# Tile 0's norm on all partitions by halves in a three-stage kernel: float32 products with ones, and reordered start steps

## The chip, the cores and the metric

The kernel runs on one core of a Trainium2 chip. The metric is the time of one execution on the device in microseconds. Engines are named as the profile names them: PE is TensorE (PEld its weight loads), DVE is VectorE, ACT is ScalarE, POOL is GpSimd, SP is SyncE, whose queue issues most DMAs.

## What is computed

Three stages follow each other: a chunked scan over four sequences with eight heads (768 tokens, 32 values a head, a state of 16), a gated feed-forward network with an RMS norm ahead of it (256 to 1536 and back), and a second network with mixed neighbours, squared ReLU and a sigmoid gate. Cut to what matters here:

```python
def _attn_ref(x, a, B, C):
    ...
        cum = np.cumsum(la, axis=-1)
        L = np.exp(cum[:, :, :, None] - cum[:, :, None, :])
        M = np.einsum('bhin,bhjn->bhij', Cc, Bc) * (L * causal)
        y_intra = np.einsum('bhij,bhjd->bhid', M, xc)
    ...

def _moe_ref(x, w_gate, w_val, w_out, rms_g):
    rms = np.sqrt(np.mean(x * x, axis=-1, keepdims=True) + 1e-06)
    xn = x / rms * rms_g
    g = xn @ w_gate
    silu = g * (1.0 / (1.0 + np.exp(-g)))
    val = xn @ w_val
    return (silu * val @ w_out).astype(np.float32)
```

All inputs and outputs are float32.

## The kernel before

The 3072 tokens go through in six tiles of 512, a tile being 128 positions of all four batches. The kernel keeps activations transposed: 128 features on partitions, 512 tokens along the row. A matrix product is made of three float32r products (`mm3`, L746): high weights by high activations, low by high, high by low; so each weight is converted, cast to a high part and differenced to a low one (`convert`, L253: `move` on DVE, two ACT steps in `magnitude`, `merge` on DVE, casts on ACT and differences on DVE in `parts`). Weights come in pairs of jobs, each pair a DMA into a `wst` tile; the casts' outputs are `wgh`, `wgl`, `wvh`, `wvl`, `woh`, `wol`.

Before the first feed-forward product of tile 0 there is a start of some 25 us. For tile 0 and tile 1 the decay matrices `E` are made on the chip: a product with an identity (`spread_eye`, L376) and a spread product with `wvvh` and `wkh` (`spread_e`, L385, the tiles are borrowed from later weights) fill a bank `Eb`, and ACT takes its exponential (`exp_e`, L399). Score products `sc` (`scores`, L468) times `E` give the mask products `M` on DVE (`mask`, L509); `M` times `x` gives `y` for one batch (`y_mm`, L536). Then comes tile 0's norm, and with it the normalised activations `xn`.

The norm of tile 0 before the change (L641 to L737): after each batch ACT squares `y` (`sq`), and two float32 products of `sq`'s columns as weights with one column of ones put the sums of 128 tokens into one column of a bank `ss`: the tokens are then on partitions. For two batches together (a half, `cols[h]`), ACT takes Ln, Exp and Square of two columns (`rms_a`, L688), DVE refines the inverse root in a Newton step (`rms_rest`, `rms_b`), and TensorE spreads each column over all partitions by a float32 product with an identity (L720). Behind the spreads of a half stands one filling product (`fill`, L635) whose result is not used. `xn_f` (L725) multiplies by the weights `g_v` and the spread factor out of the bank, `xn_split` makes the high and low parts.

`ffn1` (L752) takes tile 0's first two units (`HALVED`) in halves of 256 tokens: 48 half-width products, then units of 12 full products each, `g` and `v`, into the four banks of the pool `pmm`; ACT takes the Silu of `g` (`sl`), DVE multiplies by `v` (`hf`), and the contraction products `x` run two units behind. The attention of tile 1 runs between: `y_two` (L563) multiplies the state by `Ch`, which DVE has scaled in `ch_mul` (L495).

The order is made in two steps. `START` (L40) names the start's steps in the order in which their instructions are recorded: `e0` and `e2` exponentials of two batches, `s0` and `s1` scores, `m` masks, `y` product and square of a batch, `n` norm of a half, `c` and `P` steps of the first weight pair, `z` the next pair, `x0`, `x2` tile 1's exponentials, `S0` and `M` its scores and masks, `q0`, `q1` the identity products ahead of the first spread. A planner (`Order`, L1140) then runs all instructions through a model of engines, queues and buffers, by rank, with those of some steps marked urgent, and `arrange` (L1364) fixes each engine's order by what it found. A step that moves in `START` so moves instructions on all engines, far behind it too.

Of the kernel before, what the change touches and what calls it, by code (L numbers as in the profile page):

```python
# [9 lines left out]
F32 = mybir.dt.float32  # L10
# [3 lines left out]
AF = mybir.ActivationFunctionType  # L14
ALU = mybir.AluOpType

P = 128
NB, NH, S, D, N = 4, 8, 768, 32, 16
# [3 lines left out]
T = NB * P  # L22
# [14 lines left out]
        (99, 99, 99, 99, 99, 99, 99, 99, 99, 99, 99, 99, 99))  # L37

HIGH_ACT = ((0, 1, 2, 3, 4, 5, 6, 7, 10, 11), (2, 7))
START = 's0 k0 q0 q1 l0 p0 e0 l1 p1 m0 m1 e2 s1 m2 m3 y0 y1 y2 n0 c0 c1 P0 y3 x0 x2 d0 L0 u0 L1 n1 P1 z0 t0 S0 M1 k1 M0'  # L40
SPARE, LATE_E, BEHIND = ((0, 0), (0, 1), (1, 0)), (), (('n0', 'n1'),)
LOW_POOL, ON_POOL = (), ()

SUB_DVE, MIX_UNIT = tuple(range(27)), 9
MEANS, SPREAD, LOAD_E = (6, 10), 11, (3, 6)
WARM, COLD, HALVED, FILL = (9,), 11, 2, {('n', 0): 1, ('n', 2): 1}

TABLES = {AF.Ln: "natural_log_exp_and_others", AF.Exp: "natural_log_exp_and_others",
          AF.Silu: "silu_and_others", AF.Sigmoid: "sigmoid_and_others"}
# [28 lines left out]
def tile_kernel(ctx: ExitStack, tc, a_c, x_t, B_t, B_s, C_s, B_p, C_p, C_h, kc,  # L78
                w_gate, w_val, w_out, w_k, w_v, w_r, out):
    nc = tc.nc  # L80
    slots, chains, groups, gates, urgent, ranks, costs = {}, [], [], [], [], {}, {}
# [13 lines left out]
    rp = Pool("rp", 1)  # L95
    dp = ctx.enter_context(tc.tile_pool(name="dp", bufs=1, space=bass.MemoryType.DRAM))
    pacc = Pool("pacc", 2, bass.MemoryType.PSUM)
    pmm = Pool("pmm", 4, bass.MemoryType.PSUM)
    patt = Pool("patt", 2, bass.MemoryType.PSUM)
    vec_e, act_e, pool_e = nc.vector, nc.scalar, nc.gpsimd  # L100

    def t2(name, dt=F32, tag="t2"):
        return rp.tile([P, T], dt, tag=tag, bufs=5, name=name)
# [12 lines left out]
    def f32(ap):  # L116
        return ap.bitcast(F32)
# [27 lines left out]
    last = [None, None]  # L145
# [11 lines left out]
    def kcol(j):  # L157
        return k_sb[:, j:j + 1]
# [3 lines left out]
    ones = wp.tile([P, P], F32R, name="ones")  # L162
# [59 lines left out]
    for q in range(NU // 2):  # L222
        s = slice(2 * P * q, 2 * P * (q + 1))
# [81 lines left out]
    A = {c: {} for c in range(NC + 2)}  # L305
# [70 lines left out]
    def spread_eye(c, b):  # L376
        for half in range(2):
            pool, tag = (pacc, "acc") if c and b in LATE_E else (pmm, "mm")
            ps = A[c]["Eb", b, half] = pool.tile([P, T], F32, tag=tag, name="Eb")
            mm = nc.tensor.matmul(ps, eye, before.unsqueeze(1).broadcast_to([P, 4, P]), start=True, stop=False)  # L380
            if len(costs) < COLD:
                costs[mm.ins.name] = 427.0
            A[c]["eye", b, half] = mm.ins.name
# [171 lines left out]
    def columns_of(c, s):  # L555
        t = A[c]["yT"]
        if c:
            return t[:, :, s]
        return t.rearrange("p s (a i) -> p s a i", a=2)[:, s.start // (2 * P)]
# [67 lines left out]
    tiny = rp.tile([P, 4, P], F32, tag="Bs", bufs=1, name="tiny")  # L627
# [4 lines left out]
        nc.gpsimd.affine_select(out=eye_f, in_=eye_f, pattern=[[1, P]], base=0, channel_multiplier=-1,  # L632
                                compare_op=ALU.not_equal, fill=1.0)

    def fill(ps, n, behind):  # L635
        for k in range(n):
            mm = nc.tensor.matmul(ps, f32(ones), f32(ones).unsqueeze(1).broadcast_to([P, 2, P]), start=True, stop=True, skip_group_check=True)
            costs[mm.ins.name] = 430.0
            chains.extend((one, mm.ins.name) for one in behind)

    def square0(b):  # L641
        d = A[0]
        if b % 2 == 0:
            q = rp.tile([P, T], F32, tag="Ch", bufs=1, name="sq") if b else t2("sq")
            d["q", b // 2] = q.rearrange("p (a i) -> p a i", a=2)
            pool, tag = (patt, "at") if b else (pmm, "mm")
            d["ss", cols[b // 2].start] = pool.tile([P, T], F32, tag=tag, name="ss")
        fill(d["ss", cols[b // 2].start][:, :2 * P], FILL.get(("y", b), 0), d["last", b])
        i = slice(b % 2 * P, b % 2 * P + P)
        q, ss = d["q", b // 2][:, :, i], d["ss", cols[b // 2].start]  # L650
        nc.scalar.activation(out=q, in_=d["y", b][:, :2 * P].rearrange("p (a i) -> p a i", a=2), func=AF.Square)
        for j in range(2):
            nc.tensor.matmul(ss[:, T - NB + b:T - NB + b + 1], q[:, j], f32(ones)[:, 0:1], start=j == 0, stop=j == 1)

    def rms_sq(c, s, he, le):
        d = A[c]
# [31 lines left out]
    def rms_a(c, s):  # L688
        d = A[c]
        if c > 1:  # L690
            ss, r = d["ss", 0 if c else s.start][:, s], d["rs", 0 if c else s.start][:, s]
            ms, w = (t2(n)[:, s] for n in ("ms", "nw"))
        else:
            b = slice(s.start // P, s.stop // P)
            ss = d["ss", 0 if c else s.start][:, T - NB:][:, b]
            r, ms, w = (tiny[:, 1, 16 * c + 4 * k:16 * c + 4 * k + 4][:, b] for k in range(3))
        d["nw", s.start] = ss, r, ms, w
        tabled(out=r, in_=ss, func=AF.Ln, scale=1.0 / DM, bias=kcol(EPS))
        if c:
            rms_rest(c, s)  # L700
        tabled(out=r, in_=r, func=AF.Exp, scale=-0.5)
        tabled(out=w, in_=r, func=AF.Square)

    def rms_rest(c, s):
        ss, _, ms, _ = A[c]["nw", s.start]
        nc.vector.tensor_scalar(out=ms, in0=ss, scalar1=1.0 / DM, scalar2=1e-6, op0=ALU.mult, op1=ALU.add)

    def rms_b(c, s):
        d = A[c]
        _, r, ms, w = d.pop(("nw", s.start))  # L710
        nc.vector.scalar_tensor_tensor(out=w, in0=w, scalar=-0.5, in1=ms, op0=ALU.mult, op1=ALU.mult)
        nc.vector.scalar_tensor_tensor(out=r, in0=w, scalar=1.5, in1=r, op0=ALU.add, op1=ALU.mult)
        if c <= 1:
            if c:
                d["rs", 0 if c else s.start] = pmm.tile([P, T], F32, tag="mm", name="rb")
            else:
                d["rs", 0 if c else s.start] = d["ss", 0 if c else s.start]
            for k in range(s.stop // P - s.start // P):
                b = s.start // P + k if c else k
                mm = nc.tensor.matmul(d["rs", 0 if c else s.start][:, b * P:b * P + P], r[:, k:k + 1].broadcast_to([P, P]), eye_f,  # L720
                                 start=True, stop=True)
            if c == 0:
                fill(d["rs", s.start][:, 2 * P:], FILL.get(("n", s.start // P), 0), [mm.ins.name])

    def xn_f(c, half, s):  # L725
        d = A[c]
        if ("xnf", half) not in d:
            d["xnf", half] = t2("xnf")
        f = d["xnf", half, s.start] = d["xnf", half][:, s]
        nc.vector.scalar_tensor_tensor(out=f, in0=columns_of(c, s)[:, half], scalar=g_v[:, half:half + 1],  # L730
                                       in1=d["rs", 0 if c else s.start][:, s] if c else d["rs", 0 if c else s.start][:, :s.stop - s.start], op0=ALU.mult, op1=ALU.mult)

    def xn_split(c, half, s, he, le):
        d = A[c]
        if ("xn", half) not in d:
            d["xn", half] = pair("xn", "xn")
        split(d["xn", half][:, :, s], d.pop(("xnf", half, s.start)), he, le)  # L737

    def xn_out(c, halves, s, he, le):
        for half in halves:  # L740
            xn_f(c, half, s)
        for half in halves:
            xn_split(c, half, s, he, le)
# [146 lines left out]
    full, cols = slice(0, T), (slice(0, T // 2), slice(T // 2, T))  # L890
    nc.vector.memset(f32(ones), 1.0)

    def warm_up(n, pool, tag):
        w = pool.tile([P, T], F32, tag=tag, name="warm")
        for k in range(n):
            mm = nc.tensor.matmul(w, ones, ones.unsqueeze(1).broadcast_to([P, 4, P]), start=True, stop=True)
            if len(costs) < COLD:
                costs[mm.ins.name] = 427.0 if costs else 900.0
# [36 lines left out]
    def squares(b):  # L935
        y_mm(0, b)
        square0(b)
        y_out(0, b)

    def norms(h):  # L940
        norm0(cols[h])
# [17 lines left out]
    def late_decayed(_):  # L959
        for b in range(NB):  # L960
# [34 lines left out]
    for t in range(NC):  # L995
        c, e = t + 1, t + 2
# [105 lines left out]
        x2, tail = ffn1(t, hook)  # L1102
        if t == 0:
# [9 lines left out]
            x2 = [x2s[:, m] for m in range(2)]  # L1113
# [298 lines left out]
```

## Time and profile before

| | us |
|---|---|
| median of 3 runs | 508.67 (508.61 to 508.83) |
| profiled execution: its own time | 508.6 |
| profiled execution: span | 506.6 |
| PE busy | 500.2 (99%) |
| DVE busy | 375.7 (74%) |
| ACT busy | 307.9 (61%) |
| POOL busy | 10.4 (2%) |

The span is the time from the first instruction to the last one's end; the execution's own time has 2.0 us more around it. Busy shares are averages: in the first 30 us the engines work in a different balance from the rest, so the start is read from timelines. A matmul's end is modelled, and matmuls overlap, so the step from one's start to the next one's start tells more than its length. A float32 product stands as two records in the trace.

### The profile page before, as it was taken

What the parts mean: (1) busy time and instruction counts of PE and PEld (TensorE: products, weight loads), DVE (VectorE), ACT (ScalarE), POOL (GpSimd) and SP (SyncE); (2) the same over time, 40 slices, a digit from 0 to 9 for tenths busy, and PEclk for the clock granted to TensorE, in tenths of its full rate; (3) what the DMA queues carried; (4) which work ended last, traced back from release to release, by engine and by line L of the source; (5) the groups of instructions that cost most, each with busy time, mean ns of one, the idle gap of its engine ahead of it and who ended that gap; (6) DMA issues with size and microseconds to landing.
All of it is one profiled execution on the core that took longest, in us unless ns stands there. A gap on an engine that the chain in (4) does not pass through costs nothing.

```text
span 506.6 us, 7497 instructions
## 1 busy us (share of the span) xinstructions
PE 500.2 (99%) x2869; PEld 406.8 (80%) x2869; DVE 375.7 (74%) x610; ACT 307.9 (61%) x509; POOL 10.4 (2%) x26
## 2 busy tenths in 40 slices
PE   8999999999999999999999999999999999999997
PEld 4687887788888888888888888888888888888885
DVE  6899998988698965479995659996628763335672
ACT  5999798566589744457763456764358643345552
POOL 1100000000010000010000010000000000000000
PEclk9999999999999999999999999999999999999999
DMA  8868755342321220152111141110000000000101
GB/s 257 230 204 276 261 175 193 105 137 93 123 85 43 78 82 13 57 174 77 42 58 68 46 162 44 65 48 36 0 1 1 18 25 1 1 1 0 42 0 42
DMA packets 23283, 42.60 MB, mean 84 GB/s; under 512 B 3136, under 2 KB 6720, under 8 KB 23248
## 3 DMA queue, kind: packets, MB, share of 16 engines
q1 hardware_dynamic: 20496, 33.41, 20.0%
q10 hardware_dynamic: 2752, 8.72, 5.1%
q8 instruction: 22, 0.36, 0.3%
q14 instruction: 13, 0.11, 0.1%
HBM read 38.52 MB, written 3.34 MB: 83 GB/s over the span
## 4 chain that ended last, share of the span: by engine, by line
PE 91%; DVE 5%; ACT 2%; issue 1%; DMA 1%; DVEq 0%; ACTq 0%
PE v L748 10%; PE v L750 10%; PE v L749 10%; PE g L748 6%; PE x L748 6%; PE x L749 6%; PE x L750 6%; PE g L749 6%; PE g L750 6%; PE kp L748 4%; PE kp L750 4%; PE kp L749 4%; PE y L527 2%; PE sc L442 1%; PE rps L750 1%; PE rps L749 1%
## 5 line engine op out<-in xcount | busy, mean ns | idle before, releaser
L792 DVE TENSOR_TENSOR hf<-sl,v 128x512 f32<-128x512 f32 x72 | 49.0, 683 | 50.0 <-PE v L750 49.5
L140 ACT CAST h<-hf 128x512 fp32r<-128x512 f32 x72 | 44.4, 617 | 60.8 <-DVE hf L792 60.7
L133 ACT ACTIVATE sl<-g 128x512 f32<-128x512 f32 x72 | 42.8, 595 | 44.9 <-PE g L750 44.6
L143 DVE TENSOR_TENSOR h<-hf,h 128x512 fp32r<-128x512 f32 x72 | 50.5, 701 | 24.1 <-ACT h L140 24.1
L748 PE MATMUL g<-xn,wgh 128*128 128x512 f32 (+1 forms) x148 | 58.0, 392 | 0.4 <-DVE E L514 0.4
L749 PE MATMUL g<-xn,wgl 128*128 128x512 f32 (+1 forms) x148 | 57.0, 385 | 0.4 <-DVE wgl L289 0.4
L748 PE MATMUL v<-xn,wvh 128*128 128x512 f32 (+1 forms) x148 | 57.0, 385 | 0.0
L750 PE MATMUL g<-xn,wgh 128*128 128x512 f32 (+1 forms) x148 | 56.8, 384 | 0.0
L749 PE MATMUL v<-xn,wvl 128*128 128x512 f32 (+1 forms) x148 | 56.8, 384 | 0.0
L750 PE MATMUL v<-xn,wvh 128*128 128x512 f32 (+1 forms) x148 | 56.8, 383 | 0.0
L749 PE MATMUL x<-h,wol 128*128 128x512 f32 x144 | 56.3, 391 | 0.0
L748 PE MATMUL x<-h,woh 128*128 128x512 f32 x144 | 55.8, 391 | 0.1
L750 PE MATMUL x<-h,woh 128*128 128x512 f32 x144 | 55.2, 389 | 0.0
L867 DVE TENSOR_TENSOR k<-rl 128x512 f32<-128x512 f32 x40 | 30.0, 749 | 15.0 <-ACT rl L863 15.0
L143 DVE TENSOR_TENSOR h<-k,h 128x512 fp32r<-128x512 f32 x48 | 32.8, 686 | 10.3 <-ACT h L140 9.9
L140 ACT CAST h<-k 128x512 fp32r<-128x512 f32 x48 | 29.7, 619 | 16.5 <-DVE k L867 16.3
L748 PE MATMUL kp<-xm,wkh 128*128 128x512 f32 x96 | 37.7, 393 | 0.0
L750 PE MATMUL kp<-xm,wkh 128*128 128x512 f32 x96 | 37.4, 390 | 0.0
L749 PE MATMUL kp<-xm,wkl 128*128 128x512 f32 x96 | 37.4, 389 | 0.0
L748 PE MATMUL v<-h,wvvh 128*128 128x512 f32 x96 | 37.3, 389 | 0.0
L749 PE MATMUL v<-h,wvvl 128*128 128x512 f32 x96 | 37.3, 389 | 0.0
L863 ACT ACTIVATE rl<-kp 128x512 f32<-128x512 f32 x48 | 28.5, 594 | 14.1 <-PE kp L750 13.4
(157 smaller groups left out, 983.0 us busy)
## 6 DMA issues: line engine op xcount, KB each, us to landing
E<-la_r ACTq DMA_DIRECT2D x16, 512.0 KB
x<-in_x_t SPq DMA_DIRECT2D x6, 512.0 KB
wst<-in_w_gate SPq DMA_DIRECT2D x6, 512.0 KB
wst<-in_w_val SPq DMA_DIRECT2D x6, 512.0 KB
wst<-in_w_out SPq DMA_DIRECT2D x6, 512.0 KB
Br<-in_B_s SPq DMA_DIRECT2D x12, 256.0 KB
Cr<-in_C_s SPq DMA_DIRECT2D x12, 256.0 KB
out<-r SPq DMA_DIRECT2D x11, 256.0 KB
```

What stands on the lines that cost most here:

```text
L133: one = nc.scalar.activation(out=out, in_=in_, func=func, **kw).ins.name
L140: last[1] = nc.scalar.copy(x[:, 0, :], src).ins
L143: last[0] = le.tensor_tensor(out=x[:, 1, :], in0=src, in1=f32(x[:, 0, :]), op=ALU.subtract).ins
L442: nc.tensor.matmul(bank[:, q * 256:(q + 1) * 256], bs[:, p, :], cs[:, p, :, :].rearrange("p a i -> p (a i)"), start=True, stop=True)
L527: nc.tensor.matmul(y[half][32 * j:32 * j + 32, at[half]:at[half] + P], x[:, b, h * D:(h + 1) * D], m[:, h, :], start=start and at[half] == ...
L748: nc.tensor.matmul(ps[:, s], w[0][:, k, ws], x[:, 0, s], start=first, stop=False, skip_group_check=s.stop - s.start < T)
L749: nc.tensor.matmul(ps[:, s], w[1][:, k, ws], x[:, 0, s], start=False, stop=False, skip_group_check=s.stop - s.start < T)
L750: nc.tensor.matmul(ps[:, s], w[0][:, k, ws], x[:, 1, s], start=False, stop=last, skip_group_check=s.stop - s.start < T)
L792: nc.vector.tensor_mul(hf, sl, v)
L863: marks.append(nc.scalar.activation(out=rl, in_=kp, func=AF.Relu).ins.name)
L867: nc.vector.tensor_mul(k2, rl, rl)
```

## The change

The norm of tile 0 is made on all partitions. For each half, two float32 products of a 128 by 128 block of ones with 256 columns of squares put the sum of each token on every partition of a bank `ss`; Ln, Exp, Square and the Newton step then run on 256 columns in place of two, and `xn_f` reads the factor from SBUF (`rs`). The eight one-column products, the four spreads and the two filling products are gone. `rms_rest` now stands in `rms_a` for tile 0 as for the others. `START` has another order: the identity products first, the exponentials of the first two batches ahead of the scores, the first conversion step and the second norm half elsewhere. The diff:

```diff
-START = 's0 k0 q0 q1 l0 p0 e0 l1 p1 m0 m1 e2 s1 m2 m3 y0 y1 y2 n0 c0 c1 P0 y3 x0 x2 d0 L0 u0 L1 n1 P1 z0 t0 S0 M1 k1 M0'
+START = 'q0 q1 l0 p0 e0 l1 k0 s0 m0 m1 e2 s1 m2 c0 m3 y0 p1 y1 y2 n0 c1 P0 y3 n1 x0 x2 P1 d0 L0 u0 L1 z0 t0 S0 M1 k1 M0'
...
-WARM, COLD, HALVED, FILL = (9,), 11, 2, {('n', 0): 1, ('n', 2): 1}
+WARM, COLD, HALVED = (9,), 11, 2
...
     def square0(b):
-        d = A[0]
+        d, h = A[0], b // 2
...
-        fill(d["ss", cols[b // 2].start][:, :2 * P], FILL.get(("y", b), 0), d["last", b])
         i = slice(b % 2 * P, b % 2 * P + P)
-        nc.scalar.activation(out=q, in_=d["y", b][:, :2 * P].rearrange("p (a i) -> p a i", a=2), func=AF.Square)
-        for j in range(2):
-            nc.tensor.matmul(ss[:, T - NB + b:T - NB + b + 1], q[:, j], f32(ones)[:, 0:1], start=j == 0, stop=j == 1)
+        nc.scalar.activation(out=d["q", h][:, :, i], in_=d["y", b][:, :2 * P].rearrange("p (a i) -> p a i", a=2), func=AF.Square)
+        if b % 2:
+            pool, tag = (patt, "at") if h else (pmm, "mm")
+            ss = d["ss", cols[h].start] = pool.tile([P, T], F32, tag=tag, name="ss")
+            for j in range(2):
+                nc.tensor.matmul(ss[:, :2 * P], f32(ones), d["q", h][:, j], start=j == 0, stop=j == 1)
...
-            r, ms, w = (tiny[:, 1, 16 * c + 4 * k:16 * c + 4 * k + 4][:, b] for k in range(3))
+            if c == 0:
+                if s.start == 0:
+                    d["rs"] = rp.tile([P, T], F32, tag="rs", bufs=1, name="rs")
+                ss, r = d["ss", s.start][:, :2 * P], d["rs"][:, s]
+                ms, w = d["ss", s.start][:, 2 * P:], d["q", s.start * 2 // T][:, 0]
+            else:
+                r, ms, w = (tiny[:, 1, 16 * c + 4 * k:16 * c + 4 * k + 4][:, b] for k in range(3))
         d["nw", s.start] = ss, r, ms, w
         tabled(out=r, in_=ss, func=AF.Ln, scale=1.0 / DM, bias=kcol(EPS))
-        if c:
-            rms_rest(c, s)
+        rms_rest(c, s)
...
-            if c == 0:
-                fill(d["rs", s.start][:, 2 * P:], FILL.get(("n", s.start // P), 0), [mm.ins.name])
...
-                                       in1=d["rs", 0 if c else s.start][:, s] if c else d["rs", 0 if c else s.start][:, :s.stop - s.start], op0=ALU.mult, op1=ALU.mult)
+                                       in1=d["rs", 0][:, s] if c else d["rs"][:, s], op0=ALU.mult, op1=ALU.mult)
...
     def norm0(s):
         rms_a(0, s)
-        rms_rest(0, s)
         rms_b(0, s)
```

What this does to the engines' orders is shown at three places. A row is a line, an operation, what it writes and reads, the shape it writes, and how often it stands there in a row. Lines of the change are 8 less at the end of the file than before, and 7 less in the middle.

First, TensorE's beginning, from the warming products to the first spread products `Eb<-wvvh,wkh`. Before:

```order
L896 MATMUL warm<-ones 128x512 x9
L380 LDWEIGHTS eye
L380 MATMUL Eb<-before,eye 128x512
L476 MATMUL sc<-Cr,Br 128x256 x8
L380 LDWEIGHTS eye
L380 MATMUL Eb<-before,eye 128x512
L380 LDWEIGHTS eye
L380 MATMUL Eb<-before,eye 128x512
L380 LDWEIGHTS eye
L380 MATMUL Eb<-before,eye 128x512
L393 MATMUL Eb<-wvvh,wkh 128x512 x4
```

With the change:

```order
L889 MATMUL warm<-ones 128x512 x9
L380 LDWEIGHTS eye
L380 MATMUL Eb<-before,eye 128x512
L380 LDWEIGHTS eye
L380 MATMUL Eb<-before,eye 128x512
L380 LDWEIGHTS eye
L380 MATMUL Eb<-before,eye 128x512
L380 LDWEIGHTS eye
L380 MATMUL Eb<-before,eye 128x512
L393 MATMUL Eb<-wvvh,wkh 128x512 x4
L476 MATMUL sc<-Cr,Br 128x256 x8
```

All four identity products and the spreads now stand ahead of the eight score products `sc`; three identity products and the spreads stood behind them.

Second, ScalarE around the table load that precedes tile 0's first Silu (`sl<-g`); `wst_137` is the second weight pair, `wst_314` and `wst_307` the third. Before:

```order
L133 ACTIVATE E<-Eb 128x512 x4
L140 CAST xn<-xnf 128x256
L273 ACTIVATE wt_146<-wst_137 128x1024
L125 ACT_TABLE_LOAD
L133 ACTIVATE sl<-g 128x512
L288 CAST wgh<-wt_146 128x2x256
L288 CAST wvh<-wt_146 128x2x256
L275 ACTIVATE wst_314<-wst_314 128x1024
L133 ACTIVATE sl<-g 128x512
```

With the change:

```order
L133 ACTIVATE E<-Eb 128x512 x3
L273 ACTIVATE wt_146<-wst_137 128x1024
L275 ACTIVATE wst_137<-wst_137 128x1024
L125 ACT_TABLE_LOAD
L275 ACTIVATE wst_307<-wst_307 128x1024
L288 CAST wgh<-wt_146 128x2x256
L288 CAST wvh<-wt_146 128x2x256
L133 ACTIVATE sl<-g 128x512
L273 ACTIVATE wt_522<-wst_307 128x1024
L133 ACTIVATE sl<-g 128x512
```

The second pair's two casts and the third pair's first step now stand ahead of the first Silu; they stood behind it.

Third, VectorE from the multiplication `hf` of the first units to the scaling of `Ch` (L496). `wt_531` and `wt_522` are the third weight pair, `wt_541` is the fourth. Before:

```order
L289 TENSOR_TENSOR wgl<-wt_146,wgh 128x2x256
L289 TENSOR_TENSOR wvl<-wt_146,wvh 128x2x256
L792 TENSOR_TENSOR hf<-sl,v 128x512
L268 TENSOR_SCALAR wst_314<-wst_314 128x1024
L792 TENSOR_TENSOR hf<-sl,v 128x512
L143 TENSOR_TENSOR h<-hf,h 128x512
L496 TENSOR_TENSOR Ch<-Ch,decay 128x512
L279 SCALAR_TENSOR_TENSOR wt_531<-wt_531,wst_314 128x1024
L143 TENSOR_TENSOR h<-hf,h 128x512
```

With the change:

```order
L785 TENSOR_TENSOR hf<-sl,v 128x512
L279 SCALAR_TENSOR_TENSOR wt_522<-wt_522,wst_307 128x1024
L143 TENSOR_TENSOR h<-hf,h 128x512
L785 TENSOR_TENSOR hf<-sl,v 128x512
L289 TENSOR_TENSOR wol<-wt_522,woh 128x512 x2
L143 TENSOR_TENSOR h<-hf,h 128x512
L268 TENSOR_SCALAR wst_418<-wst_418 128x1024
L492 SCALAR_TENSOR_TENSOR decay<-decay,lmask 128x516
L506 TENSOR_TENSOR Bd<-Bt,E 128x128
L279 SCALAR_TENSOR_TENSOR wt_541<-wt_541,wst_418 128x1024
L496 TENSOR_TENSOR Ch<-Ch,decay 128x512
L186 TENSOR_SCALAR a_sb<-a_sb 48x512
```

Two merges (`wt<-wt,wst`), the two differences `wol`, a second `h`, the clip of the fourth pair's `wst_418`, the scan of `decay` and one `Bd` now stand between the first `hf` and `Ch`; the scan stood earlier in the order before.

## Rows read from the trace of the kernel before

**Rows 1.** The page's chain of work that ended last: shares by engine.

```profile
PE 91%; DVE 5%; ACT 2%; issue 1%; DMA 1%; DVEq 0%; ACTq 0%
```

**Rows 2.** Waits of TensorE: line, releaser, us in total, times, longest.

```profile
PE g L748 <- DVE E L514: 0.4, 1, 0.4
```

**Rows 3.** Timeline of TensorE: start us, us, instruction, count, idle before and releaser.

```profile
1.05 4.21 PE L896 MATMUL warm<-ones 128*128 128x512 f32 x9 [1.05 <-DVE carry L978]
...
5.43 1.59 PE L476 MATMUL sc<-Cr,Br 32*128 32x256 f32 x16
...
7.71 0.73 PE L393 MATMUL Eb<-wvvh,wkh 32*128 32x512 f32 x4
...
11.35 0.65 PE L527 MATMUL y<-M,x 128*32 128x128 f32 x16
...
24.88 0.39 PE L748 MATMUL g<-xn,wgh 128*128 128x256 f32 x1
...
30.74 0.39 PE L748 MATMUL g<-xn,wgh 128*128 128x512 f32 x1
31.50 0.50 PE L749 MATMUL g<-xn,wgl 128*128 128x512 f32 x1 [0.37 <-DVE wgl L289]
31.84 0.39 PE L750 MATMUL g<-xn,wgh 128*128 128x512 f32 x1
32.07 0.40 PE L748 MATMUL g<-xn,wgh 128*128 128x512 f32 x1
```

**Rows 4.** Timeline of ScalarE (ACT), from its first work to the first Silu.

```profile
5.99 0.69 ACT L372 ACTIVATE wkh<-hv,k_sb 128x128 fp32r<-128x128 f32 x2
...
8.23 2.06 ACT L133 ACTIVATE E<-Eb 128x512 f32<-128x512 f32 x4 [1.22 <-PE Eb L393]
10.70 2.06 ACT L133 ACTIVATE E<-Eb 128x512 f32<-128x512 f32 x4 [0.41 <-PE Eb L393]
12.63 0.42 ACT L651 ACTIVATE sq<-y 128x256 f32<-128x256 f32 x1
...
14.44 0.38 ACT L651 ACTIVATE sq<-y 128x256 f32<-128x256 f32 x1
...
15.53 0.28 ACT L133 ACTIVATE tiny<-ss,k_sb 128x2 f32<-128x2 f32 x1
15.84 0.44 ACT L133 ACTIVATE tiny<-tiny 128x2 f32<-128x2 f32 x2
...
22.64 1.16 ACT L275 ACTIVATE wst<-wst 128x1024 int32<-128x1024 uint32 x1
...
28.78 0.60 ACT L133 ACTIVATE sl<-g 128x512 f32<-128x512 f32 x1
29.27 0.61 ACT L288 CAST wgh<-wt 128x512 fp32r<-128x512 f32 x1
```

**Rows 5.** Timeline of VectorE (DVE), from 15 to 38 us.

```profile
15.56 0.68 DVE L268 TENSOR_SCALAR wst<-wst 128x1024 f32<-128x1024 f32 x1
16.16 0.15 DVE L706 TENSOR_SCALAR tiny<-ss 128x2 f32<-128x2 f32 x1
...
19.41 0.48 DVE L730 SCALAR_TENSOR_TENSOR xnf<-yT,k_sb,ss 128x256 f32<-128x256 f32 x1
...
27.91 1.22 DVE L279 SCALAR_TENSOR_TENSOR wt<-wt,wst 128x1024 int32<-128x1024 int32 x1
...
34.37 0.69 DVE L496 TENSOR_TENSOR Ch<-Ch,decay 128x512 f32<-128x512 f32 x1
...
37.31 1.29 DVE L289 TENSOR_TENSOR wol<-wt,woh 128x512 fp32r<-128x512 f32 x2
```

**Rows 6.** Timeline of TensorE: two products between two pieces of the state products.

```profile
37.38 0.73 PE L748 MATMUL x<-h,woh 128*128 128x512 f32 x2
```

**Rows 7.** One window: its us, each engine's busy us (instructions), PEclk, DMA, GB/s.

```profile
37.03:55.82 18.79, 18.79 (x126) 14.08 (x126) 18.05 (x32) 16.62 (x26) 0.00 (x0) 1.00 0.82 269
```

**Rows 8.** The page's granted TensorE clock in 40 slices, in tenths.

```profile
PEclk9999999999999999999999999999999999999999
```

More of the change, by code (lines that the diff above doesn't have):

```diff
@@ L633, in norm_eye @@
                                 compare_op=ALU.not_equal, fill=1.0)
[L635 to L639, printed above, removed]
     def square0(b):
-        d = A[0]
+        d, h = A[0], b // 2
         if b % 2 == 0:
             q = rp.tile([P, T], F32, tag="Ch", bufs=1, name="sq") if b else t2("sq")
-            d["q", b // 2] = q.rearrange("p (a i) -> p a i", a=2)
-            pool, tag = (patt, "at") if b else (pmm, "mm")
-            d["ss", cols[b // 2].start] = pool.tile([P, T], F32, tag=tag, name="ss")
-        fill(d["ss", cols[b // 2].start][:, :2 * P], FILL.get(("y", b), 0), d["last", b])
+            d["q", h] = q.rearrange("p (a i) -> p a i", a=2)
         i = slice(b % 2 * P, b % 2 * P + P)
-        q, ss = d["q", b // 2][:, :, i], d["ss", cols[b // 2].start]
-        nc.scalar.activation(out=q, in_=d["y", b][:, :2 * P].rearrange("p (a i) -> p a i", a=2), func=AF.Square)
-        for j in range(2):
-            nc.tensor.matmul(ss[:, T - NB + b:T - NB + b + 1], q[:, j], f32(ones)[:, 0:1], start=j == 0, stop=j == 1)
+        nc.scalar.activation(out=d["q", h][:, :, i], in_=d["y", b][:, :2 * P].rearrange("p (a i) -> p a i", a=2), func=AF.Square)
[4 more added lines that the diff above has]
+                nc.tensor.matmul(ss[:, :2 * P], f32(ones), d["q", h][:, j], start=j == 0, stop=j == 1)
     def rms_sq(c, s, he, le):
@@ L712, in rms_b @@
         nc.vector.scalar_tensor_tensor(out=r, in0=w, scalar=1.5, in1=r, op0=ALU.add, op1=ALU.mult)
[L713 to L717, printed above, removed]
+        if c == 1:
+            d["rs", 0] = pmm.tile([P, T], F32, tag="mm", name="rb")
             for k in range(s.stop // P - s.start // P):
-                b = s.start // P + k if c else k
+                b = s.start // P + k
                 mm = nc.tensor.matmul(d["rs", 0 if c else s.start][:, b * P:b * P + P], r[:, k:k + 1].broadcast_to([P, P]), eye_f,
                                  start=True, stop=True)
-            if c == 0:
-                fill(d["rs", s.start][:, 2 * P:], FILL.get(("n", s.start // P), 0), [mm.ins.name])
     def xn_f(c, half, s):
```

## The prediction, made before the changed kernel ran

> **What bounds the kernel now.** I read the chain of waits first, then TensorE's waits, then the timelines of the first 40 us, engine by engine. The chain that ended last is TensorE for 91% [rows 1]. So the time is the moment at which TensorE gets its dense feed-forward products, plus the products, plus whatever it waits behind them. Such waits are few: behind the start the whole run has two of 0.4 us, both on VectorE [rows 2, 3]. One stands at unit 2 of tile 0's first layer: its first product starts at 30.74, the next only at 31.50, when VectorE has the low weights `wgl` [rows 3]; at 0.23 us a product (31.84 to 32.07), 0.53 us are lost there.
>
> The timelines of the other two engines show what sets the start. ScalarE's has no wait over 0.05 us between its first squaring at 12.63 and the first Silu at 28.78 [rows 4]: 16.15 us in one piece. VectorE is nearly as full. TensorE in this stretch only looks busy; it runs short products that come when the other two have made their inputs. The reader should see that in the first 30 us a microsecond of ScalarE or VectorE work ahead of a hand-over counts, and one of TensorE hardly does.
>
> A difference under 0.2%, 1.0 us, can't be told from no change. The sum is made against the profiled execution: 508.6 us, span 506.6 and 2.0 around it. It is 0.07 under the median of the runs, so nothing is corrected. In a row of instructions that don't wait, each begins about 0.1 before the one ahead has ended (28.78 and 0.60, next at 29.27) [rows 4]; where I price an instruction in such a row, it is the row's time less 0.1.
>
> **Part 1: the spread products go ahead of the scores.** Their operand `wkh` is ready at 6.68 (5.99 and 0.69) [rows 4], yet they start at 7.71, behind the scores that run from 5.43 and three identity products [rows 3]. In the changed order they come straight behind the identity products, so at about 6.75, and the first exponential at 7.2, where it was 8.23. That 1.0 us does not last: the scores (1.5 us) now stand between these spreads and those of the other two batches, so the second four exponentials start at about 10.2, where they were at 10.70 [rows 4]. I take 0.5 us for the first squaring, 12.63 to 12.1; the bound above is the whole 1.0.
>
> **Part 2: ScalarE up to the first Silu.** Taken away: two chains of Ln, Exp and Square on two columns, of 0.75 us each (15.53 to the end at 16.28) [rows 4]: -1.5. Added: six functions of 256 columns. The nearest row is the squaring of that width, 0.38, so 0.28 in a row: 1.7 for six. Where one reads the result of the one just before it, the overlap of 0.1 is lost and 0.03 more (15.53 and 0.28, next at 15.84); that is three times, 0.4: together 2.1. Bounds: 1.3, if they cost as the narrow ones do, and 2.5, if nothing overlaps. Moved ahead of the Silu: the third weight pair's `wst` step, 1.1 by the row at 22.64, and the second pair's two casts, now behind the Silu at 29.27, 0.5 each [rows 4]: +2.1. One new wait: the second squaring needs the second batch's `y`. TensorE is through with the spreads at about 10.7, then come `y` 0.6, the other scores 1.5 and `y` 0.6 [rows 3]: 13.4, while ScalarE is free at 12.7: +0.7 (bounds 0 and 1.0). Silu(0) starts at 12.1 + 16.15 - 1.5 + 2.1 + 2.1 + 0.7 = 31.65 and ends at 32.25.
>
> [...]
>
> **Part 3: what TensorE makes of it.** The product pool `pmm` has four banks; `g` and `v` of units 0 and 1 hold all four, so the first product of unit 2 waits for Silu(0) to release one. Before, the Silu was over at 29.4 and TensorE came at 30.74. Now TensorE comes at about 31: its first dense product, 24.88 before [rows 3], stands at about 23.9 (bounds 23.5 and 24.9: the exponentials give up to 1.0, the wider norm takes some back), then come 5.8 us of half-width products and the 1.5 of tile 1's first scores, moved behind that first product. Within the bounds it comes at 30.8 to 32.2, ahead of 32.25 in every case. So what TensorE itself gains or loses in the norm (four float32 products of 256 columns for eight of one column, four spreads and two fillings) I cost at nothing: the wait for the Silu hides it. If the Silu came early, that cover would be gone and TensorE's own 31 would count. Unit 2 starts at 32.25, against 30.74 and the 0.53 lost right behind it: **+1.0 us** (bounds 0.1, with the early values of part 2, and 1.5).
>
> **Part 4: VectorE up to the state product.** `Ch` is multiplied at 34.37 [rows 5]. In the changed order there stand ahead of it, beyond what stood there: two merges of weights at 1.1, two differences `wol` (1.2 together), one more `h` at 0.6 (as wide as `Ch`'s own 0.69) and one clip of weights at 0.6: 4.6. The norm adds two scalings and four products of 256 columns, by the `xnf` row at 0.38 each, with 0.3 of waits for their own results, 2.6; it loses six narrow ones near 0.2, 1.1 [rows 5]. That makes 34.37 + 6.1 = 40.5, done at 41.2 (0.6 earlier, if the mask products keep what the exponentials give them). TensorE comes to the product of `Ch` after 36 products of unit 2, unit 3 and the first contractions: 32.25 + 36 x 0.23 = 40.5. It waits: **+0.7 us** (bounds 0 and 1.4).
>
> **Part 5: the rest.** Before, the state products were cut into four pieces among the others; two products between two pieces took 0.73 us, where two take 0.23 + 0.39 [rows 6]. The change has them in one piece: **-0.3** (0 to -0.4). Behind it VectorE has little to recover with: in 37.03 to 55.82 it was busy 18.05 of 18.79 us [rows 7]. So one more wait at a unit's product is likely until about 62 us: **+0.3** (0 to 1.0). The SP queue's order is nearly kept; `w_out` goes ahead of `x` and `Ch`, which serves the moved `wst` step and costs nothing while `Ch`'s multiplication is as late as 40.5. From unit 9 of tile 0 on TensorE's order is the same row by row, and the wait on `E` [rows 2] stays, as VectorE is late by as much.
>
> Sum: +1.0 + 0.7 - 0.3 + 0.3 = +1.7, so **510.3 us**.
>
> **Rivals.**
> - **Faster: the Silu is not the last to come.** If the exponentials keep the whole 1.0 and the wide functions cost as the narrow ones, the Silu is over near 31. The point that decides: it ends before TensorE has done its own 31, and `Ch` is done before 40. For it speak the 1.0 us that the spreads gain; against it, 2.1 us of moved work on an engine without gaps. Then unit 2 starts at 31 less up to 0.5 from the first product, 0.8 ahead of the old 30.74 and 0.53, and with the pieces put together the kernel gains 1.1: 507.5 us. Chance 0.09.
> - **Nothing to be seen.** One of the two waits falls away (parts 2 and 4 at their lower bounds, one at a time): +0.3 to +0.9, 509.2 us. Chance 0.16.
> - **The clock.** With the two fillings gone and tile 1's exponentials behind the norm on ScalarE, TensorE has 1 to 2 us without work while ScalarE does the norm (the 2.1 of part 2, in which no exponential frees a bank), and short products until its first dense one. [...] No fall in mid-kernel is in this trace. Chance 0.1.
>
> **How the numbers follow.** The forecast has 0.65; with the clock, 0.75 is slower. Range: down to 508.6, well into the middle case, up to 512.0, where unit 2 stands at +1.5, the state product's wait at 0.8, the later one at 1.0 and the pieces give nothing (a late unit 2 shortens the wait behind it, so the upper bounds don't all hold at once). The faster case and the slow end of the clock's stay out.
>
> **What would show it.** In the changed profile: first exponential near 7.2; first dense product near 24; Silu(0) ending near 32.2, with TensorE's largest later wait at the first product of unit 2, released by ScalarE; another before the product of `Ch`, released by VectorE. Wrong if unit 2's product starts before 31.3, if no wait on `Ch` shows, or if the granted clock falls.

## The result, and the profile after

| | before | changed |
|---|---|---|
| median of 7 runs | 508.78 (508.35 to 508.88) | 511.86 (509.74 to 512.77) |
| ratio | | 1.0053 (95% interval 1.0038 to 1.0067) |
| profiled execution: own time, span | 508.6, 506.6 | 512.77, 510.6 |
| chain, PE's share | 91% | 85% |

The kernel got slower by 2.7 us by the ratio; 1.7 us were forecast. The time lies inside the stated range, but at its end, and its runs spread over 3.0 us where those of before spread over 0.5. The page points at a cause: its row of the granted clock, full in all 40 slices before [rows 8], has two slices under 0.9, and part of the chain has moved from TensorE to the other engines.

```profile
PEclk9889999999999999999999999999999999999999
PE 85%; DVE 7%; ACT 4%; DMA 2%; issue 1%; SPq 1%; DVEq 0%; ACTq 0%
```

In windows of the changed kernel (columns as in rows 7: us, busy us of PE, PEld, DVE, ACT, POOL, PEclk, DMA, GB/s), TensorE is busy for 2.53 of the 4 us from 18 to 22, and then the clock falls to half:

```profile
18.00:20.00 2.00, 1.23 (x35) 0.77 (x35) 1.85 (x5) 1.91 (x6) 0.00 (x0) 1.00 0.45 133
20.00:22.00 2.00, 1.30 (x5) 0.40 (x5) 1.93 (x5) 2.00 (x6) 0.00 (x0) 1.00 0.78 194
22.00:24.00 2.00, 1.76 (x7) 0.49 (x5) 1.51 (x5) 1.80 (x5) 0.00 (x0) 0.62 1.01 380
24.00:26.00 2.00, 2.00 (x8) 1.56 (x9) 1.67 (x6) 2.00 (x6) 0.00 (x0) 0.50 0.96 340
28.00:30.00 2.00, 2.00 (x20) 1.35 (x19) 0.00 (x0) 1.97 (x3) 0.00 (x0) 0.67 0.04 8
30.00:32.00 2.00, 2.00 (x21) 2.00 (x18) 1.94 (x3) 0.85 (x1) 0.00 (x0) 1.00 0.12 27
```

TensorE's timeline of the same execution shows the idle time ahead of the fall and what came of it:

```profile
18.58 0.65 PE L533 MATMUL u<-x,Bd 128*32 128x64 f32 x32
20.70 0.38 PE L380 MATMUL Eb<-before,eye 128*128 128x512 bf16 x1 [1.47 <-ACT E L133]
...
24.62 0.58 PE L741 MATMUL g<-xn,wgh 128*128 128x256 f32 x1
...
28.20 0.41 PE L742 MATMUL g<-xn,wgl 128*128 128x256 f32 x1
28.54 1.50 PE L476 MATMUL sc<-Cr,Br 32*128 32x256 f32 x16
...
34.21 0.50 PE L741 MATMUL g<-xn,wgh 128*128 128x512 f32 x1 [0.26 <-ACT sl L133]
...
43.97 0.71 PE L569 MATMUL y<-Ch,Sf 64*128 64x128 f32 x8 [0.70 <-DVE Ch L496]
```

Between the state products `u` and the next identity product TensorE waits 1.47 us for an exponential, which stands behind the norm on ScalarE. The dense products then run at a granted clock of 0.50: from the first to the 17th it is 3.6 us (24.62 to 28.20), behind the first 0.21 from one to the next, where 0.12 is their pace at full clock (25.10 to 25.22 in before). So tile 1's first scores come at 28.54, and they are on the way to the Silu after all. VectorE waits for them, its merge of the second weight pair stands behind their masks, and ScalarE waits for the merge before it gets to the casts and Silu(0). VectorE, then ScalarE:

```profile
30.06 1.29 DVE L514 TENSOR_TENSOR E<-sc,E 128x512 f32<-128x512 f32 x2 [2.52 <-PE sc L476]
31.27 1.22 DVE L279 SCALAR_TENSOR_TENSOR wt<-wt,wst 128x1024 int32<-128x1024 int32 x1
```

```profile
32.52 0.62 ACT L288 CAST wgh<-wt 128x512 fp32r<-128x512 f32 x1 [1.67 <-DVE wt L279]
33.05 0.61 ACT L288 CAST wvh<-wt 128x512 fp32r<-128x512 f32 x1
33.57 0.59 ACT L133 ACTIVATE sl<-g 128x512 f32<-128x512 f32 x1
```

Every run lists its mean granted clock. I call a run full from 0.998 up: in the windows of two such executions whose mean is under 1.0, the clock falls only behind the last product (narrow_new_order, 0.998: 1.00 up to 505 us and 0.50 from 506; fill_clip, 0.999: 1.00 up to 504 and 0.50 from 505). Of the seven runs two are full, at 509.74 and 510.39; the five others (0.993 to 0.997) took 511.35 to 512.77. One run of the kernel before, in the sets below, took 1011.98 us at full clock and stands in no count. So the forecast's 510.3 is the time of a run that keeps its clock, and most runs don't. The experiments had to show two things: that the idle time is what lets the clock fall, and that the forecast's own terms are what is left without it.

### The profile page after: what moved, and what is told of

It reads as the page before. It is cut to its first block, busy times and chain, and to the rows that moved or that the text cites. A ratio compares the mean times of both kernels' runs of the same rounds, so it can differ in the third digit from the quotient of the medians.

```text
span 510.6 us, 7450 instructions
## 1 busy us (share of the span) xinstructions
PE 500.4 (98%) x2849; PEld 406.5 (80%) x2849; DVE 377.3 (74%) x610; ACT 308.6 (60%) x509; POOL 11.4 (2%) x26
## 4 chain that ended last, share of the span: by engine, by line
PE 85%; DVE 7%; ACT 4%; DMA 2%; issue 1%; SPq 1%; DVEq 0%; ACTq 0%
PE v L741 10%; PE v L742 10%; PE v L743 10%; PE g L741 6%; PE g L742 5%; PE x L741 5%; PE g L743 5%; PE x L742 5%; PE x L743 5%; PE kp L741 4%; PE kp L742 4%; PE kp L743 4%; PE y L527 2%; DVE wt L279 2%; DMA decay<-la_d 1%; PE sc L442 1%
## 5 line engine op out<-in xcount | busy, mean ns | idle before, releaser
L741 PE MATMUL g<-xn,wgh 128*128 128x512 f32 (+1 forms) x148 | 58.7, 396 | 0.7 <-DVE E L514 0.4
L743 PE MATMUL g<-xn,wgh 128*128 128x512 f32 (+1 forms) x148 | 57.3, 387 | 0.0
```

Of the source, the lines that this page charges most:

```text
L741: nc.tensor.matmul(ps[:, s], w[0][:, k, ws], x[:, 0, s], start=first, stop=False, skip_group_check=s.stop - s.start < T)
L743: nc.tensor.matmul(ps[:, s], w[0][:, k, ws], x[:, 1, s], start=False, stop=last, skip_group_check=s.stop - s.start < T)
```

## The experiments

Twelve kernels, in three sets, each set on one chip and beside the kernel before. "Fallen" is a run whose clock is under 0.998.

| kernel | median of all | full runs: number, median | fallen: number, range | ratio to before (interval) |
|---|---|---|---|---|
| before, all sets | 508.61 to 508.70 | 56, 508.5 to 508.6 | 11, 509.56 to 512.59 | |
| wide_fill | 511.86 | 1, 510.42 | 5, 511.55 to 513.78 | 1.0065 (1.0047 to 1.0083) |
| no_fill | 508.69 | 9, 508.46 | 3, 509.79 to 515.51 | 1.0009 (0.9983 to 1.0036) |
| wide_old_order | 511.69 | 3, 511.28 | 3, 511.83 to 513.46 | 1.0065 (1.0051 to 1.0078) |
| narrow_new_order | 511.08 | 3, 509.06 | 4, 511.08 to 512.04 | 1.0036 (1.0019 to 1.0054) |
| fill_a | 509.46 | 11, 509.45 | 1, 511.56 | 1.0015 (1.0005 to 1.0026) |
| fill_b | 509.96 | 9, 509.96 | 0 | 1.0027 (1.0017 to 1.0037) |
| fill_merge | 510.59 | 5, 510.59 | 0 | 1.0038 (1.0025 to 1.0051) |
| fill_merge_ch | 511.51 | 5, 511.51 | 0 | 1.0057 (1.0045 to 1.0070) |
| after_again | 511.52 | 2, 510.51 | 4, 511.13 to 513.91 | 1.0056 (1.0035 to 1.0076) |
| fill_one | 511.36 | 5, 509.60 | 7, 511.20 to 513.78 | 1.0045 (1.0027 to 1.0063) |
| fill_clip | 508.44 | 11, 508.44 | 0 | 0.9994 (0.9986 to 1.0003) |
| narrow_front | 509.49 | 7, 509.35 | 5, 512.27 to 513.64 | 1.0036 (1.0014 to 1.0057) |

**wide_fill: three filling products in the norm's own bank.**

```diff
...
         rms_rest(c, s)
+        if c == 0 and s.start:
+            fill(ss, 3)
...
```

Other lines, not shown here, hold the three behind the last product `u`.

> The changed kernel with three filling float32 products (128 by 256, result unused) put behind the state products u, where TensorE stood idle for 1.47 us at 19.23; the order of every engine is otherwise the same. Theory 1 (the clock): the granted clock fell at 22.48 because TensorE had too little to do ahead of it, and the half-rate products to 29.31 cost 2 to 3 us. Then the clock is 1.0 in every run, the first dense product stays at 24.6, unit 2's first product comes at 32 to 32.7 instead of 34.21, and the time is 509.7 to 510.4, the value of the changed kernel's two runs with a clock of 1.0, with a spread under 0.7 us. Theory 2 (the lists alone: the late Silu and the late Ch set the time, and the clock is a bystander): unit 2's first product stays near 34 and the time at 511.9, or 0.3 above it.

The gap at 19.23 was filled, and yet the clock fell in five runs of six. The experiment was spoilt by its place: the Newton step shares the bank and waited for the fills (19.02 to 20.58), and a new gap stood behind it, right ahead of the fall at 24.4 (the clock is 0.70 from 24 to 25 us and 0.50 from 25 to 26; TensorE's timeline):

```profile
24.26 0.48 PE L380 MATMUL Eb<-before,eye 128*128 128x512 bf16 x1 [1.28 <-ACT E L133]
```

**fill_a: the same three products into a free bank.** `FILL` names the step, the product of it behind which they go, and their number; `moves` puts an instruction behind another in the planned order, and changes nothing else in it.

```diff
+FILL = (('u0', -1, 3),)
...
+        if step == "S0":
+            idle = pacc.tile([P, T], F32, tag="acc", name="idle")
+            for one in FILL:
+                fill(*one, idle)
...
-    _, order = o.run()
+    _, order = o.run()
+    for one, ref, behind in moves:
+        order.remove(where[one])
+        order.insert(order.index(where[ref]) + behind, where[one])
```

> The changed kernel with three filling float32 products behind the state products u, now into a bank that nothing near it uses (in wide_fill they sat in the norm's own bank, the Newton step waited for them, the first dense product came 0.8 us later and TensorE was idle for 1.28 us at 22.98). The order of all engines is otherwise the same. Theory 1 (the clock falls because of the idle 1.47 us at 19.23): clock 0.998 to 1.0 in at least two runs of three, those at 509.6 to 510.4 us, and the median there too; no idle of TensorE over 0.5 us between 17 and 25. Theory 2 (these idle times are not what decides; the whole stretch up to the first dense product is too thin): the clock falls in most runs as in the changed kernel, and the median stays at 511.5 to 512.

Eleven runs of twelve are full, and the median falls to 509.46. TensorE's work in the same windows, with the clock full:

```profile
18.00:20.00 2.00, 2.00 (x40) 1.61 (x39) 1.95 (x6) 1.91 (x6) 0.00 (x0) 1.00 0.56 162
20.00:22.00 2.00, 1.76 (x8) 0.43 (x6) 1.59 (x4) 2.00 (x6) 0.00 (x0) 1.00 0.54 135
22.00:24.00 2.00, 1.71 (x8) 0.76 (x8) 1.77 (x5) 2.00 (x6) 0.00 (x0) 1.00 0.98 320
```

**fill_b: three more.**

```diff
-FILL = (('u0', -1, 3),)
+FILL = (('u0', -1, 3), ('x0', 7, 1), ('x2', 1, 1), ('x2', 5, 1))
```

> As fill_a, with three more filling products, one each behind later spread and identity products (up to 0.43 us each, so the first dense product may come up to 0.6 us later). Theory 1: as fill_a, clock 1.0 in nearly every run, 509.7 to 510.8 us. Theory 2 (the stretch behind 20.7 is what is too thin): clock 1.0 in nearly every run here, though not in fill_a. If filling has nothing to do with the clock, it falls as often as in the changed kernel, in five runs of seven, and the median is near 512.

Nine of nine are full, but the first dense product comes at 24.56 (23.71 in fill_a; 0.2 of that stands from the first exponential on, 7.09 for 6.86), and the time is 0.5 higher. Three were enough.

**fill_one: one product in place of three.**

```diff
-FILL = (('u0', -1, 3),)
+FILL = (('u0', -1, 1),)
```

> fill_a with one filling product in place of three, so about 1.0 us without work left where the changed kernel has 1.5 and fill_a none. If idle time of TensorE ahead of the first dense product decides on the clock: it falls in fewer runs than in the changed kernel and in more than in fill_a (one of twelve); full-clock runs 509.3 to 509.8, fallen ones 511.3 to 512.8. If a product there, of whatever length, is enough: as fill_a.

Seven of twelve fall. That is more than fill_a's one of twelve, but it can't be told from the changed kernel's 9 of 13 below: one product is not shown to help. Its profiled execution fell (own time 513.09); its longest wait for an exponential is 0.8 us, and TensorE did less than in fill_a:

```profile
18.00:20.00 2.00, 1.81 (x37) 1.07 (x37) 1.90 (x5) 1.91 (x6) 0.00 (x0) 1.00 0.59 186
20.00:22.00 2.00, 1.34 (x5) 0.40 (x5) 1.93 (x5) 2.00 (x6) 0.00 (x0) 1.00 0.48 107
22.00:24.00 2.00, 1.49 (x6) 0.44 (x5) 1.50 (x5) 2.00 (x6) 0.00 (x0) 0.72 0.98 343
```

The full runs are at 509.60, near fill_a's 509.45: two products more cost nothing that shows.

**after_again: the changed kernel, on the chip of fill_one and fill_clip.**

> The changed kernel once more, on the same chip as the other three of this set, to count how often the granted clock falls. If the falls belong to the kernel: in over half of the runs the clock is 0.997 or less and the time 511.3 to 512.8; the others take 509.4 to 510.4. If they belonged to the chip it ran on before: clock 1.0 in nearly all and 509.4 to 510.4.

Four of six fall. With the seven runs of the result that is 9 of 13 for the changed kernel; for all kernels with three or more fills in the free bank (fill_a, fill_b, fill_merge, fill_merge_ch, fill_clip) it is 1 of 42, and fill_clip, on this very chip, has 0 of 11. So the falls belong to the kernel, and three products in the idle time behind `u` all but end them (fill_a itself ran on another chip, and fill_clip has less VectorE work as well). The median of its 9 fallen runs is 512.14, of its 4 full ones 510.26: a fall costs 1.9 us.

The profiled execution of after_again kept its clock (own time 510.13). TensorE:

```profile
20.85 0.38 PE L380 MATMUL Eb<-before,eye 128*128 128x512 bf16 x1 [1.47 <-ACT E L133]
...
24.27 0.38 PE L741 MATMUL g<-xn,wgh 128*128 128x256 f32 x1
...
26.49 1.15 PE L476 MATMUL sc<-Cr,Br 32*128 32x256 f32 x16
...
32.29 0.50 PE L741 MATMUL g<-xn,wgh 128*128 128x512 f32 x1 [0.76 <-ACT sl L133]
32.63 0.40 PE L742 MATMUL g<-xn,wgl 128*128 128x512 f32 x1
...
41.56 0.71 PE L569 MATMUL y<-Ch,Sf 64*128 64x128 f32 x8 [0.66 <-DVE Ch L496]
...
58.84 0.39 PE L742 MATMUL g<-xn,wgl 128*128 128x512 f32 x1
...
62.16 0.50 PE L741 MATMUL v<-xn,wvh 128*128 128x512 f32 x1 [0.43 <-ACT sl L133]
```

ScalarE:

```profile
5.26 0.69 ACT L372 ACTIVATE wkh<-hv,k_sb 128x128 fp32r<-128x128 f32 x2
...
7.52 2.06 ACT L133 ACTIVATE E<-Eb 128x512 f32<-128x512 f32 x4 [1.24 <-PE Eb L393]
9.97 2.32 ACT L133 ACTIVATE E<-Eb 128x512 f32<-128x512 f32 x4 [0.39 <-PE Eb L393]
12.17 0.40 ACT L641 ACTIVATE sq<-y 128x256 f32<-128x256 f32 x1
...
13.21 0.38 ACT L641 ACTIVATE sq<-y 128x256 f32<-128x256 f32 x1 [0.37 <-PE y L527]
...
17.71 0.95 ACT L133 ACTIVATE rs<-ss,k_sb 128x256 f32<-128x256 f32 x2
...
20.22 1.07 ACT L133 ACTIVATE E<-Eb 128x512 f32<-128x512 f32 x2
...
31.65 0.59 ACT L133 ACTIVATE sl<-g 128x512 f32<-128x512 f32 x1
```

The same 1.47 us of idle time stand here, and the clock did not fall. The shortage is in both profiled executions, the fall in one.

**no_fill: the fills of before cut to two columns.**

```diff
-            mm = nc.tensor.matmul(ps, f32(ones), f32(ones).unsqueeze(1).broadcast_to([P, 2, P]), start=True, stop=True, skip_group_check=True)
+            mm = nc.tensor.matmul(ps[:, :2], f32(ones), f32(ones)[:, :2], start=True, stop=True, skip_group_check=True)
```

> The kernel before, its two filling products cut from 256 columns to 2, in the same place; the order of every engine is the same. Theory 1a (the two filling products are what holds the clock): the granted clock falls in some runs, and these take 510 to 512 us. Theory 1b (the one-column products and spreads of the old norm, or the shorter idle times, hold the clock without them): clock 1.0 in every run, 508.5 to 508.9 us, no difference.

Three of twelve fall, against 11 of 67 in the kernel before itself (these two counts can't be told apart) and 9 of 13 in the changed one. The loss of these two products alone does not explain the falls. The surprise is that before falls too, by itself, in one run of six.

**wide_old_order and narrow_new_order: norm and order apart.** Only the line `START` is exchanged: in the changed kernel as shown, in the kernel before the other way round.

```diff
-START = 'q0 q1 l0 p0 e0 l1 k0 s0 m0 m1 e2 s1 m2 c0 m3 y0 p1 y1 y2 n0 c1 P0 y3 n1 x0 x2 P1 d0 L0 u0 L1 z0 t0 S0 M1 k1 M0'
+START = 's0 k0 q0 q1 l0 p0 e0 l1 p1 m0 m1 e2 s1 m2 m3 y0 y1 y2 n0 c0 c1 P0 y3 x0 x2 d0 L0 u0 L1 n1 P1 z0 t0 S0 M1 k1 M0'
```

> The changed kernel's norm on all partitions, with the START of the kernel before (so the scores ahead of the spreads; the planner still puts the second pair's casts and the third pair's step ahead of the first Silu). Theory 1 (the clock): the norm starves TensorE with either START, so the clock falls in some or all runs, and these take 510.5 to 513 us. Theory 2 (the reordered start costs, as the prediction had it): clock 1.0, and the time is between 508.6 and 509.2 us.

> The kernel before, its norm on columns and its two filling products, with the changed START. Theory 1 (the clock falls for want of work in the wide norm): clock 1.0 in every run. Theory 2 (the reordered start costs 1 to 1.7 us by the wait for Silu(0) and for Ch, whatever the norm): 509.7 to 510.4 us; if the START costs nothing, 508.4 to 509.0 us.

With the old order the wide norm is the worst of all, 511.28 in full runs: the first dense product waits for its own input (TensorE's timeline).

```profile
27.16 0.39 PE L741 MATMUL g<-xn,wgh 128*128 128x256 f32 x1 [1.41 <-ACT xn L140]
```

So the wide norm with the old `START` costs 2.7 at full clock, where 508.6 to 509.2 was expected, and the reordering pays 1.0 of it back (511.28 to 510.26; three and four runs). The new `START` with the old norm costs 0.5 at full clock (509.06), under the expected 1.0 to 1.7, and its clock falls in four runs of seven, where none was expected: the falls are not the wide norm's doing alone, as I had it. The split is not clean, as the planner makes a new order of all engines each time: in both kernels the second pair's casts stand ahead of the first Silu (31.44 and 32.47 us in wide_old_order; by ScalarE's order of instructions in narrow_new_order).

**narrow_front: the front of the new order alone**, identity products and spreads ahead of the first scores, in the kernel before.

```diff
-START = 's0 k0 q0 q1 l0 p0 e0 l1 p1 m0 m1 e2 s1 m2 m3 y0 y1 y2 n0 c0 c1 P0 y3 x0 x2 d0 L0 u0 L1 n1 P1 z0 t0 S0 M1 k1 M0'
+START = 'q0 q1 l0 p0 e0 l1 k0 s0 p1 m0 m1 e2 s1 m2 m3 y0 y1 y2 n0 c0 c1 P0 y3 x0 x2 d0 L0 u0 L1 n1 P1 z0 t0 S0 M1 k1 M0'
```

> The kernel before, with its norm on columns and its filling products, and of the changed START only the front: identity products and spreads ahead of the first scores. Prediction, part 1 alone: the first exponential at 7.2, the second four near 10.2, the first squaring 0.5 earlier. If that carries through, the first dense product comes 0.5 earlier and the time is 508.0 to 508.4 at full clock; if the scores and masks behind it give it back, 508.4 to 509.2. The clock: full as often as before, if the norm is what starves TensorE; often fallen, as in narrow_new_order, if the new front does.

The exponentials come early (7.43 for the first) and the first dense product 0.7 earlier than before, but tile 1's first scores now stand behind it, the second product of unit 2 is no earlier (31.50 before [rows 3]), and a wait for VectorE follows (TensorE's timeline):

```profile
24.15 0.47 PE L748 MATMUL g<-xn,wgh 128*128 128x256 f32 x1
...
25.74 1.15 PE L476 MATMUL sc<-Cr,Br 32*128 32x256 f32 x16
...
31.58 0.40 PE L749 MATMUL g<-xn,wgl 128*128 128x512 f32 x1
...
38.27 0.50 PE L749 MATMUL x<-h,wol 128*128 128x512 f32 x1 [0.42 <-DVE wol L289]
```

So the front's gain is given back; the full runs take 509.35, 0.8 more than before. Five of twelve fall, at 512.27 and over, and idle time is not shown to be the reason: in the profiled execution, which kept its clock, TensorE has no wait of 0.2 us or more between the warming products and the first dense one (in fill_a it is busy for 5.47 of the 6.00 us from 18 to 24). No fallen run of this kernel has a profile, so where its clock falls, and why, is open.

**fill_merge and fill_merge_ch: the waits of parts 2 and 4 taken away.**

```diff
+    moves.append((seen["merge", 2], seen["mask", 1, 0, 0], 0))
+    moves.append((seen["wl", 2, 0], seen["mask", 1, 1, 1], 0))
+    moves.append((seen["wl", 2, 1], seen["mask", 1, 1, 1], 0))
+    moves.append((seen["low", 4], seen["silu", 0, 0], 1))
...
+    moves.append((seen["Ch", 1], seen["scan", 1], 1))
```

> As fill_a, with the second weight pair's merge ahead of tile 1's masks on VectorE, its two differences ahead of the last two masks, and the third pair's wst step behind Silu(0) on ScalarE. The prediction's part 2 (work moved ahead of the Silu makes unit 2 late by 1.0): at full clock unit 2's first product comes near 31.6 instead of 32.4, with no wait for wgl behind it; but the wait for Ch grows by what unit 2 gains, so the full-clock time falls by at most 0.5 against fill_a. Rival (the Silu is not what TensorE waits for at full clock): unit 2 starts as in fill_a and nothing moves.

> As fill_merge, with the multiplication of Ch straight behind the scan of decay on VectorE, so 1.3 us earlier. If parts 2 and 4 of the prediction hold, both waits go and the full-clock time is 1.0 to 1.8 us under fill_a's, 508.4 to 509.2. If VectorE merely pays later (the fourth pair's merge is 0.6 later), it is 509.3 to 509.9.

Unit 2 did start without a wait, at 31.17, but both kernels are slower, by 1.1 and 2.1. In fill_a the same product was:

```profile
31.73 0.50 PE L743 MATMUL g<-xn,wgh 128*128 128x512 f32 x1 [0.75 <-ACT sl L135]
```

In fill_merge the unit's first product `v` waits for VectorE's `hf`, which the moved instructions pushed to 33.40 (32.44 in fill_a), and the wait for `Ch` stays:

```profile
31.17 0.40 PE L743 MATMUL g<-xn,wgh 128*128 128x512 f32 x1
...
34.13 0.50 PE L743 MATMUL v<-xn,wvh 128*128 128x512 f32 x1 [1.42 <-DVE hf L788]
...
42.73 0.71 PE L571 MATMUL y<-Ch,Sf 64*128 64x128 f32 x8 [0.77 <-DVE Ch L498]
```

With `Ch` early as well, fill_merge_ch waits for a later unit's Silu instead:

```profile
44.87 0.50 PE L743 MATMUL g<-xn,wgh 128*128 128x512 f32 x1 [1.30 <-ACT sl L135]
```

Both expectations failed: with the lists in these two orders the wait moved from one place to the next.

**fill_clip: less work on VectorE, same order.** The clip of two weight pairs acts on 4 columns only.

```diff
...
+            if j in (4, 6):
+                hi = hi[:, :4]
...
```

> fill_a with VectorE's clip of the third and the fourth weight pair's high words cut from 1024 columns to 4 (the clip acts on extreme values only; here they stay as they are), so 1.1 us less on VectorE ahead of Ch; the order of all engines is the same. Prediction, part 4 (VectorE's list sets when Ch is there): the wait of 0.64 for Ch goes, and the time falls by 0.6 to 1.2 against fill_a's 509.46, to 508.3 to 508.9. Rival (ScalarE's list, through the casts and Silus, sets it as much): Ch is earlier, but the time falls by less than 0.3.

1.0 us under fill_a, as expected: `Ch` is multiplied 0.5 earlier (40.27 in fill_a) and its wait is gone, while the wait for Silu(0) has not changed. VectorE, then TensorE:

```profile
39.74 0.69 DVE L502 TENSOR_TENSOR Ch<-Ch,decay 128x512 f32<-128x512 f32 x1
```

```profile
32.02 0.50 PE L747 MATMUL g<-xn,wgh 128*128 128x512 f32 x1 [0.76 <-ACT sl L135]
...
40.56 0.72 PE L575 MATMUL y<-Ch,Sf 64*128 64x128 f32 x8
```

So taking work off VectorE gained what the two other orders did not. The kernel only draws level with before (0.9994, interval 0.9986 to 1.0003) by leaving part of the clip out. None of these versions that does all the work beats before.

## Why the prediction was right, and where it was wrong

| | forecast | clock kept (after_again) | clock fell (changed kernel) |
|---|---|---|---|
| first exponential | 7.2 | 7.52 | 7.27 |
| first squaring | 12.1 | 12.17 | 11.93 |
| first dense product | 23.9 | 24.27 | 24.62 |
| Silu(0) starts | 31.65 | 31.65 | 33.57 |
| unit 2's first product | 32.25 | 32.29 | 34.21 |
| `Ch` multiplied | 40.5 | 40.82 | 43.23 |
| wait for `Ch` | 0.7 | 0.66 | 0.70 |
| execution's own time | 510.3 | 510.13 | 512.77 |

- **Part 1 held in place and size** (7.52 for 7.2, 12.17 for 12.1), the first exponential in after_again partly by luck: `wkh` was ready at 5.95 there, and the identity products, which took 1.93 us, held the spreads up in its place (last section). That the front is worth nothing by itself is shown by narrow_front.
- **Part 2 held, with two sizes that cancelled.** The six wide functions took 2.51 us (17.71 to 20.22) for 2.1, at my upper bound of 2.5. The wait for the second `y` was 0.37 for 0.7.
- **Part 3: the wait of unit 2 for Silu(0) is there** (0.76, released by ScalarE). Its second product comes at 32.63, 1.1 later than in before (31.50 [rows 3]), for a forecast 1.0.
- **Part 4 held** (0.66 for 0.7), and fill_clip shows that VectorE's amount of work sets it.
- **Part 5: two sizes off, again against each other.** One and the same product of unit 4 stands 1.0 later than in before (42.62 to 43.66), and one of a later unit 0.8 (58.06 to 58.84). So of the 1.8 of the two waits (1.13 and 0.66) the pieces put together gave back about 1.0 rather than 0.3. At 62 us the later wait shows, and from 66 us on the lag is 1.4 (66.09 to 67.52): the later waits cost 0.65 for 0.3. Sum at full clock 1.4 to 1.5 for 1.7.
- **What failed is the clock rival.** I gave it 0.1. It came in 9 of 13 runs, and cost 1.9. By the last of its own signs, a granted clock that falls, the prediction is wrong in most runs. Two steps were wrong. First its chance: the clock that is full in all 40 slices [rows 8] is that of one execution, and I took it for all; before itself falls in 11 of 67. Second its cost. The range leaves out the slow end of the clock's, a term that no run of before shows; what the runs showed in its place are times of up to 513.91, and in the profile of the changed kernel a fall from 22.5 to 29.3 us, 6.8, to 0.50. And part 3 lets what TensorE loses vanish in the wait for the Silu, as if the Silu were ScalarE's affair alone. But the scores that I had moved behind the dense products feed VectorE's masks, the masks stand ahead of the merge, and the merge is ahead of the casts and of Silu(0). With the clock at 0.50 the Silu comes 1.9 later (33.57 for 31.65), so the cover moved with the loss. That the idle time was there, and that it came from the norm on ScalarE without the fills, the rival had right (1 to 2 us; 1.47 measured).

The time lies inside the range because its upper end was made from late waits; the runs got there by another way, and that is luck. That idle time of TensorE could let its clock fall was my estimate; fill_a against the changed kernel, one order with three products more, agrees with 1 fallen run in 12 against 9 in 13; narrow_front's falls no trace explains.

## What to carry to other kernels

Look for idle time of TensorE ahead of its dense stretch, not only for work on the critical path: a profile at full clock shows one execution, so read the spread and the mean clock of all runs before calling the clock safe. When an edit frees TensorE's time in a thin stretch, fill it, into a bank that nobody near it uses; here that held the clock in 41 of 42 runs, against 4 of 13 without, though no filled kernel beat the one before. And when a loss is to hide behind a wait, follow what the wait itself is made of: if it hangs on the same engine, it moves along.

## What the runs showed that I had not expected

- The same idle time, 1.47 us, stands in an execution whose clock fell and in one whose clock did not. The longest idle time ahead of the dense products does not tell the other profiles apart either: the clock fell with 1.28 us (wide_fill) and 0.8 (fill_one), and held with 1.41 (wide_old_order), 0.93 (narrow_new_order) and 0.3 (fill_a). Before, too, falls in one run of six; none of these has a profile.
- How long TensorE's products take right behind the warming ones differs from run to run as well, and the new order feels it. The four identity products there took 1.93 us in after_again and 1.04 in fill_a, with a mean granted clock of 1.0 in both (TensorE's timelines, in this order):

```profile
5.06 1.93 PE L380 MATMUL Eb<-before,eye 128*128 128x512 bf16 x4
```

```profile
5.05 1.04 PE L382 MATMUL Eb<-before,eye 128*128 128x512 bf16 x4
```

The first exponential follows (7.52 and 6.86), and 0.56 of the difference still stands at unit 2 (32.29 and 31.73). That, and not the fills, is most of what parts these two executions, 509.45 and 510.13. Whether the runs that keep their clock are those in which these four products take long is open: only one such execution of the changed kernel has a profile.
